# VectorE instead of GpSimd makes the low parts of the converted float64 weights

## The chip, the cores and the metric

One core of one Trainium2 chip runs the kernel. The metric is the device time of one execution in microseconds (us); a profiled execution has a span (first to last instruction of the program) and its own device time, which is a little longer.

## What is computed

A linear attention over 8 batches and 8 heads, followed by an MLP-mixer block:

```python
def phi(x):                       # x: q or k, (8, 8, 576, 64); w_phi: (64, 128)
    proj = einsum('bhsd,df->bhsf', x, w_phi)
    proj = proj - max(abs(proj), axis=-1)
    return concatenate([exp(proj), exp(-proj)], axis=-1)
kv  = einsum('bhsf,bhsd->bhfd', phi(k), v);  z = phi(k).sum(axis=2)
x   = einsum('bhsf,bhfd->bhsd', phi(q), kv) / (phi(q)·z + 1e-6)   # -> (8, 576, 512)
h   = relu(x^T @ w_tok1) @ w_tok2                    # 576 -> 256 -> 576
u   = x + h^T
out = u + relu(u @ w_ch1) @ w_ch2                    # 512 -> 1536 -> 512
```

The four MLP weights arrive as float64. Everything else is float32.

## The kernel before

**Split numbers.** Most products are made of float32r parts: a number is cast to float32r (the high part `hi`, on ScalarE or another engine), and the low part is `lo = raw - hi`. `mm3` (L70) then makes three matmuls, high by high, high by low, low by high. `split` (L62) is the helper that makes both parts: line L65 is the cast on ScalarE, L68 the subtraction, on the engine that the caller names.

**Weights.** `load_weights` (L137) calls `convert` once for each block of a weight: 7 blocks for `w1` and `w2` (tiles `bits`, `w_h`, `w_l`), 12 blocks of 128x512 for `wc1` (tiles `bitsc`, `wc_h`, `wc_l`) and 12 of 128x512 for `wc2` (tiles `bitsc`, `wc`: both parts lie in one tile). `convert` (L107) loads the 64-bit words with a DMA on SyncE's queue (L118) into one of four staging buffers, and turns them into float32 with integer operations: the absolute value of the upper word on ScalarE (L124), then on VectorE a clamp (L125), a shift and mask (L126), the sign and exponent (L127) and the three bits out of the lower word (L128). L125 and L126 read one tensor, `m`, the `bits` tile of the pool; L127 and L128 read two, the loaded words and `m`. `split` follows. The `bits` tile has three buffers, and one is free again when its low part has been subtracted.

**Streams.** Five generators are woven by `weave` (L547) into one program: `keys` and `queries` (the attention, one pair of heads at a time), `token_stream` (the token mix of a batch, when its attention is done), `load_weights` and `channel_stream` (18 blocks of 256 tokens). The first four pairs of heads (`i < PLAIN`) go through plain float32 matmuls, and VectorE takes their maxima (L219) and differences (`pmk`, `pmq`, L221) straight out of PSUM. From the fifth pair on the difference is GpSimd's (L221, `eng = nc.gpsimd`), and so are the low parts of keys and queries (L180), half of the low parts of the query features (L357), the division of the numerators (L402) and the low parts of the mixer's input (L470). The denominators of the first eight pairs make a round trip through DRAM (L394 to L399) with a reciprocal on VectorE between (L396).

**Order.** The kernel is built with the tile framework and `schedule_with_timeline_sim=True`: the framework plans the order of each engine's instructions by its own timeline before the launch, from the order of the woven program and the dependences; semaphores are added to that order. On the chip each engine works its list in order. In the trace the operations of up to three `convert` calls alternate on VectorE with those of the attention.

Of the kernel before, what the change touches and what calls it, by code (L numbers as in the profile page):

```python
# [8 lines left out]
F32 = mybir.dt.float32  # L9
# [33 lines left out]
def mixer_kernel(ctx, tc, qk, vm, vt, w_phi, w1, w2, wc1, wc2d, out):  # L43
    nc = tc.nc
# [17 lines left out]
    def split(hi, lo, raw, eng_hi, eng_lo):  # L62

        if eng_hi is nc.scalar:
            nc.scalar.copy(hi, raw)  # L65
        else:
            eng_hi.tensor_copy(hi, raw)
        eng_lo.tensor_tensor(lo, raw, hi.bitcast(F32), op=ALU.subtract)  # L68
# [38 lines left out]
    def convert(hi, lo, srcs, name, tag=None):  # L107

        w, n = hi.shape
        if tag is None:  # L110
            tag = f"late{nstage[0] % STAGES}"
            nstage[0] += 1
        raw = wk.tile([P, 4, 256], U32, tag=tag, name=f"raw{name}", bufs=3 if tag == "xt1" else 1)
        raw = raw.rearrange("p a b -> p (a b)")[:w, :2 * n]
        at = 0
        for src in srcs:
            m = src.shape[1]
            nc.sync.dma_start(raw[:, 2 * at:2 * (at + m)].bitcast(I64), src)  # L118
            at += m
        raw = raw.rearrange("p (n two) -> p n two", two=2)  # L120
        top, low = raw[:, :, 1], raw[:, :, 0]
        m = wk.tile([P, 512], U32, tag="bits", name=f"bits{name}", bufs=3)[:w, :n]

        nc.scalar.activation(m.bitcast(F32), top.bitcast(F32), AF.Abs)  # L124
        nc.vector.tensor_scalar(m.bitcast(F32), m.bitcast(F32), LEAST, MOST, op0=ALU.max, op1=ALU.min)  # L125
        nc.vector.tensor_scalar(m, m, 3, 0x3FFFFFF8, op0=ALU.logical_shift_left, op1=ALU.bitwise_and)  # L126
        nc.vector.scalar_tensor_tensor(m, top, 0xC0000000, m, op0=ALU.bitwise_and, op1=ALU.bitwise_or)  # L127
        nc.vector.scalar_tensor_tensor(m, low, 29, m, op0=ALU.logical_shift_right, op1=ALU.bitwise_or)  # L128
        split(hi, lo, m.bitcast(F32), nc.scalar, nc.gpsimd)

    def flat(t):
        return t.rearrange("p a b -> p (a b)")
# [4 lines left out]
    def load_weights():  # L137
        for u in (0, 3):
            s = UNITS[u][2]
            convert(flat(w1_h[:, u:u + 2]), flat(w1_l[:, u:u + 2]),  # L140
                    [w1[s + o:s + o + P] for o in (0, P)], f"1_{u}")
            yield 1.0
        convert(w1_h[:D, 2], w1_l[:D, 2], [w1[512:]], "1_2")
        for w in (w1_h, w1_l):
            nc.scalar.copy(w[D:, 2], w[:D, 2].bitcast(F32))
        yield 0.4
        for u in range(NT):
            rows = w2[u * P:(u + 1) * P]
            convert(w2_h[:, u, :256], w2_l[:, u, :256], [rows[:, :256]], f"2_{u}")
            yield 0.5  # L150
            convert(w2_h[:, u, 256:], w2_l[:, u, 256:], [rows[:, 512:], rows[:, 256:512]], f"3_{u}")
            yield 0.7
# [457 lines left out]
```

## Time and profile before

| | |
|---|---|
| device time, three runs | 1168.47, 1168.24, 1161.84 us (median 1168.24) |
| profiled execution: device time / span | 1164.33 / 1162.2 us |
| PE busy (matmul) | 1121.3 us, 96% of the span, 9032 matmuls |
| DVE / ACT / POOL busy | 685.7 / 659.4 / 570.1 us (59 / 57 / 49%) |
| chain that ended last, by engine | PE 85%, ACT 5%, DVE 4%, DMA 3%, issue 1%, POOL 1% |
| granted TensorE clock, mean | 0.992 |

PE is TensorE, PEld its weight load, DVE VectorE, ACT ScalarE, POOL GpSimd, SP SyncE. L12 is line 12 of the kernel. Times within the span count from its start. A name before the arrow is the tile that is written, names behind it are the tiles that are read.

### The profile page before, as it was taken

The page shows a single profiled execution, that of the slowest core. Times are in us where ns is not written, and L with a number is a line of the kernel's source. Part 1 is how long each engine was busy: PE and PEld are TensorE (multiplying, and loading weights), DVE is VectorE, ACT ScalarE, POOL GpSimd, SP SyncE. Part 2 cuts the span into 40 slices and gives each one's busy share as a digit, 9 for nine tenths or more (in the row PEclk, how much of TensorE's full clock was granted, in tenths as well). Part 3 has the DMA queues.
Part 4 walks back from the last instruction along what each step waited for, and adds up shares of the span by engine and source line. Part 5 has one row for each costly group of instructions (what it writes and reads, how often), then busy time and mean ns, then how long its engine had stood idle before and what let it go on. Part 6 is the DMA issues. An engine that isn't in the chain of part 4 may idle for free.

```text
span 1162.2 us, 24135 instructions
## 1 busy us (share of the span) xinstructions
PE 1121.3 (96%) x9032; PEld 1090.5 (94%) x9032; DVE 685.7 (59%) x1446; ACT 659.4 (57%) x1845; POOL 570.1 (49%) x734
## 2 busy tenths in 40 slices
PE   8987799999999999999999999999999999999998
PEld 7766699998999899999999999999999989999998
DVE  7989763536656665667566465573666666553111
ACT  5678785666656665666657465563655666441110
POOL 3347773555545564566646354563554655430000
PEclk9988999999999999999999999999999999999999
DMA  8564130111111011111111011110111110000000
GB/s 224 162 187 135 42 88 24 47 43 54 32 28 52 21 41 41 32 49 32 32 49 33 19 32 50 32 50 13 38 48 33 50 31 11 20 1 19 19 19 19
DMA packets 72531, 56.77 MB, mean 49 GB/s; under 512 B 49920, under 2 KB 63648, under 8 KB 72416
## 3 DMA queue, kind: packets, MB, share of 16 engines
q1 hardware_dynamic: 71056, 54.89, 16.7%
q8 instruction: 71, 1.16, 0.4%
q10 hardware_dynamic: 1360, 0.36, 0.2%
q14 instruction: 44, 0.36, 0.1%
HBM read 45.72 MB, written 9.51 MB: 48 GB/s over the span
## 4 chain that ended last, share of the span: by engine, by line
PE 85%; ACT 5%; DVE 4%; DMA 3%; issue 1%; POOL 1%; SPq 0%; POOLq 0%; DVEq 0%; ACTq 0%
PE acc L74 25%; PE h L74 25%; PE pkv L287 9%; PE pn L74 7%; PE ph L74 4%; PE pa L74 3%; PE pt L343 3%; PE ppk L205 2%; PE ppq L205 2%; DMA inv<-few 1%; PE px L423 1%; PE pn L377 1%; PE ppk L209 1%; ACT qh L356 1%; ACT qf L350 1%
## 5 line engine op out<-in xcount | busy, mean ns | idle before, releaser
L74 PE MATMUL acc<-gh,wc 128*128 128x256 f32 x1728 | 336.5, 282 | 0.2 <-ACT gh L489 0.2
L74 PEld LDWEIGHTS acc<-gh,wc 128*128 128x128 f32 x1728 | 274.0, 189 | 0.5 <-ACT gh L489 0.4
L74 PE MATMUL h<-ul,wc_h 128*128 128x256 f32 x864 | 243.4, 282 | 1.9 <-POOL ul L470 1.8
L74 PE MATMUL h<-uh,wc_h 128*128 128x256 f32 x864 | 244.8, 284 | 0.5 <-DVE gl L490 0.5
L74 PE MATMUL h<-uh,wc_l 128*128 128x256 f32 x864 | 243.7, 282 | 0.0
L74 PE MATMUL acc<-gl,wc 128*128 128x256 f32 x864 | 242.3, 282 | 0.0
L287 PE MATMUL pkv<-v,kp 128*128 128x65 f32 (+1 forms) x1152 | 165.7, 280 | 0.4 <-ACT kp L265 0.3
L74 PEld LDWEIGHTS h<-ul,wc_h 128*128 128x128 f32 x864 | 163.1, 189 | 2.7 <-POOL ul L470 2.7
L74 PEld LDWEIGHTS h<-uh,wc_h 128*128 128x128 f32 x864 | 162.6, 188 | 1.2 <-DVE gl L490 1.1
L74 PEld LDWEIGHTS h<-uh,wc_l 128*128 128x128 f32 x864 | 163.4, 189 | 0.0
L74 PEld LDWEIGHTS acc<-gl,wc 128*128 128x128 f32 x864 | 162.8, 188 | 0.0
L287 PEld LDWEIGHTS pkv<-v,kp 128*128 128x128 f32 x1152 | 156.9, 203 | 4.0 <-issue 1.8
L265 ACT ACTIVATE kp<-pmk 128x256 f32<-128x256 f32 (+1 forms) x320 | 109.3, 392 | 89.0 <-POOL pmk L221 83.7
L357 POOL TENSOR_TENSOR ql<-qf,qh 128x320 fp32r<-128x320 f32 (+1 forms) x112 | 92.8, 828 | 135.9 <-ACT qh L356 133.2
L490 DVE SCALAR_TENSOR_TENSOR gl<-h,gh 128x512 fp32r<-128x512 f32 x108 | 74.0, 686 | 140.3 <-ACT gh L489 139.6
L350 ACT ACTIVATE qf<-pt 128x320 f32<-128x320 f32 (+1 forms) x256 | 105.2, 414 | 84.6 <-PE pt L343 83.9
L489 ACT ACTIVATE gh<-h 128x512 fp32r<-128x512 f32 x108 | 64.6, 598 | 102.5 <-PE h L74 101.8
L74 PE MATMUL pn<-qh,kv 128*128 128x320 f32 (+1 forms) x448 | 114.9, 297 | 1.7 <-DVE pq L214 0.8
L402 POOL TENSOR_TENSOR xt<-xt,den 128x320 f32<-128x320 f32 x64 | 53.8, 840 | 116.7 <-DVE den L401 36.6
L357 DVE TENSOR_TENSOR ql<-qf,qh 128x320 fp32r<-128x320 f32 (+1 forms) x112 | 71.1, 635 | 65.0 <-ACT qh L356 64.6
L221 POOL TENSOR_TENSOR pmk<-pk,mxk 128x256 f32<-128x256 f32 (+1 forms) x140 | 86.8, 620 | 30.0 <-DVE mxk L219 23.2
L180 POOL TENSOR_TENSOR stq<-raw,stq 64x512 fp32r<-64x512 f32 (+1 forms) x56 | 79.8, 1424 | 40.5 <-ACT stq L179 36.4
(109 smaller groups left out, 2420.8 us busy)
## 6 DMA issues: line engine op xcount, KB each, us to landing
raw<-in_qk SPq DMA_DIRECT2D x27, 576.0 KB, 4.0
rawc<-in_wc SPq DMA_DIRECT2D x24, 512.0 KB, 4.8
v<-in_vm SPq DMA_DIRECT2D x31, 256.0 KB, 3.9
out_x<-xt SPq DMA_DIRECT2D x12, 256.0 KB, 2.2
out_x<-xt SPq DMA_DIRECT2D x16, 192.0 KB, 2.0
raw<-in_w SPq DMA_DIRECT2D x8, 256.0 KB, 3.5
out_x<-xt SPq DMA_DIRECT2D x16, 128.0 KB, 3.0
pair<-in_qk SPq DMA_DIRECT2D x8, 160.0 KB, 3.8
```

What stands on the lines that cost most here:

```text
L74: nc.tensor.matmul(o, a, m, start=first and i == 0, stop=last and i == 2, skip_group_check=group_ok)
L180: nc.gpsimd.tensor_tensor(t[lo:lo + D], src, t[base:base + D].bitcast(F32), op=ALU.subtract)
L205: nc.tensor.matmul(ps[:, i].rearrange("p two f -> p (two f)"), t[:, c:c + P], wp2.rearrange("p two f -> p (two f)"), start=True, stop=True)
L221: eng.tensor_tensor(pm[:, :n], pr, mx[:, :n].unsqueeze(2).to_broadcast([P, n, F]), op=ALU.subtract)
L265: nc.scalar.activation(kp[:, :len(us), sg], pm[:, :len(us)], AF.Exp, scale=1.0 - 2.0 * sg)
L287: nc.tensor.matmul(o, kp[:, n, sg], v, start=g == 0 and n == 0 and sg == 0, stop=u is None, skip_group_check=True)
L343: nc.tensor.transpose(ptr[:, n], r, ident)
L350: nc.scalar.activation(full, src, AF.Exp, scale=1.0 - 2.0 * sg)
L357: (nc.gpsimd if sg else nc.vector).tensor_tensor(lo, full, hi.bitcast(F32), op=ALU.subtract)
L402: nc.gpsimd.tensor_tensor(x, x, den, op=ALU.mult)
L489: nc.scalar.activation(gh, ph, AF.Relu)
L490: nc.vector.scalar_tensor_tensor(gl, ph, 0.0, gh.bitcast(F32), op0=ALU.max, op1=ALU.subtract)
```

## The change

In `convert`, the engine that `split` is given for the low part is VectorE instead of GpSimd. All 31 subtractions of L68 for weights move; their operands and results, and every other operation, stay as they were. The program is planned anew by the framework, since one of its instructions has another engine.

```diff
         nc.vector.scalar_tensor_tensor(m, low, 29, m, op0=ALU.logical_shift_right, op1=ALU.bitwise_or)
-        split(hi, lo, m.bitcast(F32), nc.scalar, nc.gpsimd)
+        split(hi, lo, m.bitcast(F32), nc.scalar, nc.vector)
```

## Rows read from the trace of the kernel before

**Rows 1.** Windows: stretch, length, busy us of PE, PEld, DVE, ACT, POOL, clock, DMA.

```profile
9.00:66.00 57.00, 56.70 (x234) 46.36 (x234) 52.07 (x118) 38.72 (x96) 21.52 (x16) 1.00 0.71 197
66.00:125.00 59.00, 45.85 (x250) 37.52 (x251) 55.62 (x102) 45.77 (x112) 36.84 (x30) 0.87 0.51 142
125.00:165.00 40.00, 35.84 (x275) 33.54 (x274) 25.86 (x64) 32.02 (x90) 30.42 (x38) 0.98 0.19 52
165.00:1162.00 997.00, 977.91 (x8258) 968.67 (x8257) 548.53 (x1153) 540.15 (x1545) 479.85 (x637) 1.00 0.12 33
```

**Rows 2.** The chain that ended last, 66 to 125 us: start, us, what.

```profile
75.36 3.92 DMA inv<-few
...
90.99 1.68 POOL wc L68
...
102.35 1.63 DVE bitsc L126
...
109.37 1.42 DVE bitsc L128
```

**Rows 3.** Groups by shape on DVE, 66 to 125 us: busy us, mean ns, idle before.

```profile
L128 DVE SCALAR_TENSOR_TENSOR bitsc<-rawc,bitsc 128x512 uint32<-128x512 uint32 x14 | 13.4, 959 | 0.0
L126 DVE TENSOR_SCALAR bitsc<-bitsc 128x512 uint32<-128x512 uint32 x13 | 11.4, 877 | 0.0
L127 DVE SCALAR_TENSOR_TENSOR bitsc<-rawc,bitsc 128x512 uint32<-128x512 uint32 x13 | 10.8, 831 | 0.0
L125 DVE TENSOR_SCALAR bitsc<-bitsc 128x512 f32<-128x512 f32 x13 | 8.7, 679 | 2.3 <-ACT bitsc L124 2.3
```

**Rows 4.** Tile bitsc, whole span: duration ns min/median/max, first and last start.

```profile
L126 DVE TENSOR_SCALAR bitsc<-bitsc x24: 408/424/1751, 28.9 to 156.3; 128x512 uint32<-128x512 uint32 x24
...
L128 DVE SCALAR_TENSOR_TENSOR bitsc<-rawc,bitsc x24: 645/680/1751, 31.7 to 158.2; 128x512 uint32<-128x512 uint32 x24
```

**Rows 5.** Timeline of DVE, then of POOL: start, us, engine, line.

```profile
84.80 0.69 DVE L128 SCALAR_TENSOR_TENSOR bitsc<-rawc,bitsc 128x512 uint32<-128x512 uint32 x1
85.40 0.42 DVE L126 TENSOR_SCALAR bitsc<-bitsc 128x512 uint32<-128x512 uint32 x1
...
102.27 1.71 DVE L126 TENSOR_SCALAR bitsc<-bitsc 128x512 uint32<-128x512 uint32 x1
...
102.16 1.54 POOL L180 TENSOR_TENSOR stq<-raw,stq 64x640 fp32r<-64x640 f32 x1 [1.36 <-ACT stq L179]
```

**Rows 6.** Groups by shape on POOL, 66 to 125 us.

```profile
L68 POOL TENSOR_TENSOR wc_l<-bitsc,wc_h 128x512 fp32r<-128x512 f32 x8 | 11.6, 1452 | 9.5 <-ACT wc_h L65 9.4
L68 POOL TENSOR_TENSOR wc<-bitsc,wc 128x512 fp32r<-128x512 f32 x5 | 6.9, 1379 | 1.7 <-ACT wc L65 1.6
```

**Rows 7.** Waits of DVE and POOL, 66 to 125 us: total us, times, longest.

```profile
DVE bitsc L125 <- ACT bitsc L124: 2.3, 3, 1.2
...
POOL wc_l L68 <- ACT wc_h L65: 9.4, 4, 2.9
...
POOL wc L68 <- ACT wc L65: 1.6, 2, 1.3
```

**Rows 8.** Windows of L68 alone: DVE busy, POOL busy, clock, DMA.

```profile
9.00:66.00 57.00, 0.00 (x0) 20.66 (x15) 1.00 0.71 197
...
125.00:165.00 40.00, 1.68 (x4) 3.86 (x3) 0.98 0.19 52
```

**Rows 9.** Waits of POOL, 9 to 66 us.

```profile
POOL wc L68 <- ACT wc L65: 9.2, 4, 4.2
POOL wc_l L68 <- ACT wc_h L65: 8.1, 3, 3.6
```

**Rows 10.** Timeline of PE: the two longest gaps between 66 and 125 us.

```profile
74.76 0.48 PE L209 MATMUL ppt<-wp,pair 64*128 64x128 f32 x2 [3.42 <-DVE pmq L221]
...
91.92 0.74 PE L209 MATMUL ppq<-wp,pair 64*128 64x128 f32 x4 [3.69 <-DVE pmq L221]
```

## The prediction

> **What bounds the kernel now.** I read the busy shares first, then the busy time by stretch, because a share over the whole span says nothing about the one stage that the change touches. The subtractions that move all start within the first 162 us. The windows [rows 1] show four stages. From 9 to 66 us PE is busy 56.70 of 57.00 us, and DVE 52.07. From 66 to 125 us PE falls to 45.85 of 59.00 us while DVE is busy 55.62, and TensorE's granted clock is 0.87 instead of 1.00: this is VectorE's stage. From 125 to 165 us no engine is full (PE 35.84, POOL 30.42, DVE 25.86 of 40.00). From 165 us to the end PE is busy 977.91 of 997.00 us, and since its work there stays the same, the end of the kernel is set by how much of PE's work the first 165 us could not place. So the change can act only through PE's idle time before 165 us: 59.00 − 45.85 = 13.2 us in VectorE's stage, 4.2 us behind it, next to nothing in the first stage. The chain of waits [rows 2] agrees: in 66 to 125 us it goes over denominators' round trips through DRAM, bit operations on DVE, and once over a moved operation, 1.68 us of POOL.
>
> The next view is the groups by shape in VectorE's stage against the quickest operations of the same shape. The 53 bit operations there took 13.4 + 11.4 + 10.8 + 8.7 = 44.3 us [rows 3]. Undisturbed ones take about 0.42 us (L125 and L126) and 0.68 us (L127 and L128), the medians [rows 4]; 26 x 0.42 + 27 x 0.68 = 29.3 us. So 15.0 us of VectorE's 55.62 is stretch. The timeline shows its source: a POOL subtraction started at 102.16 and took 1.54 us, and DVE's L126, started 0.11 us later, took 1.71 instead of 0.42, ending 0.28 us behind POOL [rows 5]. GpSimd's work on SBUF holds these DVE operations up.
>
> **The change part by part.**
>
> *Added to DVE.* No low part of a weight is on DVE in the trace. The nearest rows are L127 and L128, also two tensors in SBUF, 128x512: 0.68 us busy, and start to start 0.60 us where the next operation is ready (84.80 to 85.40 [rows 5]). I take 0.60 for each; at 0.68 the sum below grows by 1.0. Thirteen lie in VectorE's stage [rows 6]: +7.8 us there.
>
> *Removed stretch.* POOL is busy 36.84 us in this stage, of which the thirteen L68 are 11.6 + 6.9 = 18.5 us, one half [rows 1, 6]. I give them half of the stretch: −7.5 us. The bounds: nothing, if the remaining POOL work (which now starts earlier) meets DVE as often, and −15.0, if all of it was theirs.
>
> *New stretch.* The moved operations read two tensors in SBUF, as L127 and L128 do, so the rest of POOL's work can hold them up as well. That rest makes the other 7.5 us of stretch on 53 operations, 0.14 us each; 13 x 0.14 = +1.8 us (from 0 to 13 x 0.28 = 3.7, if stretch per operation stayed at today's 15.0 / 53).
>
> The Trainium skill, page "SBUF — State Buffer", section "SBUF: two separate sides", says that VectorE and GpSimd share one port pair as an exclusive lock, that a DVE operation with two SBUF inputs or in a two-port mode contends for it, and that whoever starts first holds it for the whole instruction. The rows at 102.16 and 102.27 agree [rows 5]. It speaks against counting the removed stretch as clear gain, since the subtraction stays a contender on its new engine; a result that the rule would allow is the second rival.
>
> *A new wait on DVE.* The subtraction needs ScalarE's cast (L65), which needs L128: a trip from DVE to ACT and back. DVE works in order, so behind a waiting L68 are queued the next bit operations and the maxima and differences (L219, L221) for which PE waits. The nearest DVE row is L125, which waits for ACT's L124: 2.3 us for thirteen [rows 7], so I take +2.3 us. It is so little because DVE has a backlog and the planner puts other work between. The other end is what POOL waits for the same cast today, 9.4 + 1.6 = 11.0 us for thirteen [rows 7]; POOL is less loaded and arrives earlier, hence DVE's row, but the end stays in the range. The lower end is 0.
>
> *Taken from POOL.* 18.5 us of work in this stage. Behind it in POOL's list stand the low parts of keys and queries (L180), L402 and L221. POOL idles 22 of 59 us, so most of this was not in the way; the one L68 in the chain is 1.68 us [rows 2]: −1.7 us (0 to −1.7). No DMA is issued by POOL here and the moved operation issues none; SyncE's load of the next block waits for L127 and L128, not for the subtraction. The `bits` buffer, freed by the subtraction, now comes free in DVE's order; ScalarE's L124 is what would wait.
>
> *Sum in VectorE's stage:* 7.8 − 7.5 + 1.8 + 2.3 − 1.7 = +2.7 us.
>
> *First stage, 9 to 66 us.* Fifteen move, among them seven smaller ones; at 0.60 at most +9.0 us, against the stretch that leaves with 20.66 us of POOL's 21.52 [rows 1, 8]. By VectorE's stage's ratio (15.0 us of stretch for 36.84 of POOL, 0.41) that is −8.4. Net +0.6, covered by PE's full stage and DVE's 4.9 us of idle time: 0. Were no stretch to leave, 9.0 − 4.9 = 4.1 us would show, the upper end; the lower end is −1, for PE has hardly a gap to give back.
>
> *Third stage.* Three move, +1.8 us on a DVE that is idle 14 of 40 us, −3.86 us on POOL, which is busy three quarters [rows 1, 8]. I take 0, between −3.9 and +1.8.
>
> *Behind 165 us* nothing moves, but the framework plans the whole program anew. PE's idle time there is 19.1 us; a third of it either way, ±6 us, is my bound for another order.
>
> The sum is +2.7 us on the profiled execution, 1164.33 to 1167.0. That execution lies 3.9 us under the median of the three runs, 1168.24; on the median the sum is 1170.9. I take the middle base, 1166.3, for everything: **1169 us**. Its own range, 1160 to 1177, has the re-planning and the bounds of the smaller terms.
>
> **Rivals.**
>
> *DVE is held at its head by ScalarE (slower).* If DVE comes to each L68 about as early as POOL does now, it inherits the 11.0 us instead of 2.3 in VectorE's stage: 1166.3 + 2.7 + 8.7 = 1177.7. In the first stage it would inherit 9.2 + 8.1 = 17.3 us [rows 9], of which 4.9 fit in its idle time: up to +12.4 more, 1190. The middle is 1184. It decides from about 0.5 us of wait for each operation on. For it: the trip to ACT is real, ACT is busy 45.77 of 59 us there and works in order. Against it: the small wait of L125 [rows 7].
>
> *POOL leaves more than its half (faster).* The removed operations hold DVE for their whole length, 18.5 us, not 7.5: −11.0 more, 1166.3 + 2.7 − 11.0 = 1158.0. (The lock that the Trainium skill's page "SBUF — State Buffer" states, section "SBUF: two separate sides", would allow this.) DVE's maxima would then come sooner, and PE's two long gaps, 3.42 and 3.69 us, both ended by `pmq` on DVE [rows 10], may close: down to 1150.9. I name 1155. Against it: the stretch that is there in all is 15.0 us, and the moved work takes 7.8 itself.
>
> *The new plan decides, the stage comes out even.* Moved work and stretch cancel, DVE's wait is nothing, and only the order behind 165 us differs: 1166.3 ± 6, 1160 to 1172. This is also the case where the change shows nothing.
>
> **How the numbers follow.** Forecast 0.48; DVE held by ScalarE 0.24; more from POOL's leaving 0.16; new plan alone 0.12. A measurement of this kernel can tell 1% from no change, 11.7 us: below 1156.6 is faster, above 1179.9 slower. Of the second rival two thirds lie below, 0.11, with 0.02 from the others: faster 0.13. Of the first rival three quarters lie above, 0.18, with 0.03 from the forecast's tail (both ends of the unknown waits together): slower 0.21. The rest, 0.66, is the same. The range leaves out a tenth on each side: the lower half of the second rival and the upper part of the first, 1154 to 1186.
>
> **What would show it.** In the changed profile, L125 to L128 in VectorE's stage should be at a mean near 0.55 to 0.75 us instead of 0.68 to 0.96; a DVE group of 24 L68 with mean 0.68 to 0.85 us; its idle time before, ended by ACT's L65, under 5 us in all (over 15 is the first rival); DVE still above 90% busy from 66 to 125 us; POOL's other subtractions unchanged in length; PE full from about 167 us on. The prediction is wrong if DVE idles in front of L68, if the stretch of the bit operations stays or disappears whole, or if PE's idle time behind 165 us differs by more than 6 us.

## The result and the profile after

The changed kernel took 1175.22 us (median of 20 runs, 1164.64 to 1180.82), the kernel before 1168.36 (20 runs). The ratio is 1.0071, 95% interval 1.0047 to 1.0095: slower by 0.7%, some 7 to 8 us. In a second comparison (`changed_again` below) the ratio was 1.0115 (1.0074 to 1.0155).

The profiled execution of the changed kernel took 1164.77 us with a span of 1163.0 us, at the quick end of its runs. So its rows show what moved, but not the loss. On its page PE has 1112.6 us (96%), DVE 693.9, ACT 657.6, POOL 528.6.

Windows of the changed kernel, the same stretches and columns as [rows 1]:

```profile
9.00:66.00 57.00, 54.65 (x289) 43.90 (x290) 49.99 (x130) 42.97 (x111) 5.27 (x5) 0.97 0.67 175
66.00:125.00 59.00, 42.74 (x253) 35.49 (x253) 53.13 (x112) 42.56 (x109) 20.72 (x23) 0.93 0.50 150
125.00:165.00 40.00, 33.29 (x208) 30.71 (x207) 37.67 (x70) 26.61 (x70) 21.12 (x23) 0.80 0.22 67
165.00:1162.00 997.00, 976.75 (x8266) 967.33 (x8265) 549.51 (x1157) 542.70 (x1552) 480.09 (x639) 1.00 0.12 33
```

Against [rows 1], TensorE does 289 matmuls instead of 234 in the first stage, about as many in the second, and 208 instead of 275 in the third. (A second execution of the same program did 261, 214 and 173, so single counts are rough.) VectorE is busier in the third stage (37.67 us instead of 25.86) and less busy in the first two (103.1 instead of 107.7). The change left no conversion work out; it is done later.

DVE groups by shape, 66 to 125 us, which answer to [rows 3], and the moved subtraction with its counts, durations (min/median/max ns) and the waits ahead of it:

```profile
L127 DVE SCALAR_TENSOR_TENSOR bitsc<-rawc,bitsc 128x512 uint32<-128x512 uint32 x12 | 9.4, 787 | 0.0
L128 DVE SCALAR_TENSOR_TENSOR bitsc<-rawc,bitsc 128x512 uint32<-128x512 uint32 x12 | 8.8, 732 | 0.0
L125 DVE TENSOR_SCALAR bitsc<-bitsc 128x512 f32<-128x512 f32 x11 | 7.2, 657 | 0.4 <-ACT bitsc L124 0.4
L126 DVE TENSOR_SCALAR bitsc<-bitsc 128x512 uint32<-128x512 uint32 x12 | 6.8, 570 | 0.0
```

```profile
L68 DVE TENSOR_TENSOR wc_l<-bitsc,wc_h x12: 644/682/1509, 38.0 to 138.9; 128x512 fp32r<-128x512 f32 x12
L68 DVE TENSOR_TENSOR wc<-bitsc,wc x12: 672/684/1609, 60.0 to 159.2; 128x512 fp32r<-128x512 f32 x12
...
  ACT xh L65: 34.8, 33
  ACT wc L65: 0.8, 2
```

The bit operations are shorter than in [rows 3], by 22 (L125) to 307 ns (L126). The subtraction takes 0.68 us on VectorE where GpSimd took 1.38 to 1.45 [rows 6], and the cast keeps VectorE waiting for 0.8 us in all (the 34.8 us above it belong to another use of the helper, `xh`). By these rows alone the change looks like a small gain. The experiments had to find where the loss comes from.

### The profile page after: what moved, and what is told of

It reads as the page before. It is cut to its first block, busy times and chain, and to the rows that moved or that the text cites. A ratio compares the mean times of both kernels' runs of the same rounds, so it can differ in the third digit from the quotient of the medians.

```text
span 1163.0 us, 24116 instructions
## 1 busy us (share of the span) xinstructions
PE 1112.6 (96%) x9032; PEld 1081.7 (93%) x9032; DVE 693.9 (60%) x1477; ACT 657.6 (57%) x1845; POOL 528.6 (45%) x703
## 4 chain that ended last, share of the span: by engine, by line
PE 82%; DVE 5%; ACT 5%; DMA 4%; issue 1%; POOL 1%; SPq 1%; DVEq 0%; POOLq 0%; ACTq 0%
PE acc L74 25%; PE h L74 24%; PE pkv L287 9%; PE pn L74 7%; PE ph L74 4%; PE pt L343 3%; PE pa L74 2%; PE ppk L205 2%; PE ppq L205 2%; DMA few<-row 2%; DMA inv<-few 1%; PE px L423 1%; PE ppk L209 1%; DMA den<-inv 1%; PE pn L377 1%
## 5 line engine op out<-in xcount | busy, mean ns | idle before, releaser
L287 PE MATMUL pkv<-v,kp 128*128 128x65 f32 (+1 forms) x1152 | 161.1, 275 | 3.2 <-ACT kp L265 2.3
L287 PEld LDWEIGHTS pkv<-v,kp 128*128 128x128 f32 x1152 | 152.0, 198 | 6.7 <-ACT kp L265 2.9
L350 ACT ACTIVATE qf<-pt 128x320 f32<-128x320 f32 (+1 forms) x256 | 105.2, 415 | 80.0 <-PE pt L343 78.6
L221 POOL TENSOR_TENSOR pmk<-pk,mxk 128x256 f32<-128x256 f32 (+1 forms) x140 | 86.6, 619 | 34.0 <-DVE mxk L219 27.9
```

The costliest lines, as they stand in the source:

```text
L221: eng.tensor_tensor(pm[:, :n], pr, mx[:, :n].unsqueeze(2).to_broadcast([P, n, F]), op=ALU.subtract)
L287: nc.tensor.matmul(o, kp[:, n, sg], v, start=g == 0 and n == 0 and sg == 0, stop=u is None, skip_group_check=True)
L350: nc.scalar.activation(full, src, AF.Exp, scale=1.0 - 2.0 * sg)
```

## Experiments

Two things change together: the engine of 31 subtractions, and the order that the framework plans for every engine. Read by line and tile from the two traces, TensorE's list of matmuls differs from the old one at some 820 of its 9032 places, nearly all between the 73rd and the 1129th; the other engines' lists differ as well. To separate the two, a kernel builds the program twice: the first build gives each engine's order, and the second is bound to it, all but the 31 subtractions, by ordering edges that need no semaphore. This code, and the edits below, are shortened:

```python
order = program(on_gpsimd, lay)[1]        # whose plan is kept
nc = program(on_vector, lay, order)[0]    # who makes the low parts
...
for names in order.values():              # or one engine's list, or a part of it
    for first, then in zip(names, names[1:]):
        tc.add_manual_dep(made[then], first, NoSync)
```

In these kernels the subtraction on VectorE has line L611 and the cast of the weights L129; the other lines keep their numbers. The table holds all runs, and the change itself as `after`. Each was timed beside the kernel before; as the four timings of that kernel differ, runs are compared by their ratios. The last two columns are added up from the windows of each profiled execution: matmuls from 9 to 165 us, and VectorE's busy time from 9 to 125 us.

| run | low part | lists kept | median us | ratio (95%) | span | PE 9–165 | DVE 9–125 |
|---|---|---|---|---|---|---|---|
| before | GpSimd | own plan | 1162.73 to 1168.97 | 1 | 1162.2 | 759 | 107.7 |
| after | VectorE | own plan | 1175.22 | 1.0071 (1.0047–1.0095) | 1163.0 | 750 | 103.1 |
| changed_again | VectorE | own plan | 1178.44 | 1.0115 (1.0074–1.0155) | 1182.0 | 648 | 91.6 |
| vector_old_order | VectorE | all old | 1159.62 | 0.9958 (0.9925–0.9991) | 1157.8 | 768 | 109.6 |
| zero_low_old_order | none | all old | 1162.32 | 0.9970 (0.9947–0.9993) | 1157.3 | 789 | 102.4 |
| gpsimd_new_order | GpSimd | all new | 1177.34 | 1.0108 (1.0069–1.0147) | 1172.4 | 683 | 91.1 |
| vector_old_dve_list | VectorE | DVE old | 1178.07 | 1.0085 (1.0053–1.0117) | 1181.0 | 637 | 94.8 |
| vector_old_pe_list | VectorE | PE old | 1163.45 | 0.9958 (0.9932–0.9985) | 1164.6 | 761 | 105.2 |
| gpsimd_new_dve_list | GpSimd | DVE new | 1177.84 | 1.0075 (1.0047–1.0104) | 1177.4 | 657 | 89.6 |
| change_five_bits | VectorE | own plan | 1173.54 | 1.0052 (1.0023–1.0080) | 1174.9 | 673 | 101.1 |
| vector_old_pe_first200 | VectorE | PE old to 200 | 1164.55 | 1.0004 (0.9977–1.0031) | 1164.9 | 773 | 108.1 |
| vector_old_pe_from200 | VectorE | PE old from 200 | 1174.12 | 1.0080 (1.0053–1.0108) | 1170.0 | 670 | 97.2 |
| gpsimd_new_pe_list | GpSimd | PE new | 1179.50 | 1.0142 (1.0099–1.0185) | 1186.1 | 582 | 89.0 |
| replanned_before | GpSimd | own plan | 1173.23 | 1.0074 (1.0043–1.0104) | 1165.9 | 753 | 108.7 |

**Work or order.** The changed kernel once more, the work without the new order, the new order without the work, and the old order with no subtraction at all (that kernel leaves the low parts out: GpSimd writes zeros in their place).

changed_again:

> The change once more, to have it on one chip beside the next three. Both theories expect what was measured, +0.5 to +1.0% against the kernel before (+6 to +11 us), and TensorE's mean granted clock lower than in the kernel before by about 0.01.

vector_old_order, `order = program(on_gpsimd)`, `nc = program(on_vector, order)`:

> The 31 subtractions on VectorE, but every other instruction of every engine in the planned order of the kernel before; only the subtractions are placed anew. Theory A (the work: 0.6 us for each on VectorE outweighs the stretch that leaves) expects +6 to +11 us against before, as for the change. Theory B (the order: the new plan loses the time, the work is even) expects within 3 us of before. My forecast of the sum, work alone, was +2.7 us.

gpsimd_new_order, against vector_old_order:

```diff
-    order = program(on_gpsimd, lay)[1]
-    nc = program(on_vector, lay, order)[0]
+    order = program(on_vector, lay)[1]
+    nc = program(on_gpsimd, lay, order)[0]
```

> The subtractions on GpSimd as before, every other instruction in the planned order of the changed kernel. Theory A expects before's time within 3 us; theory B expects +6 to +11 us. If both parts matter, this and the run with the old order add up to the change.

zero_low_old_order, against vector_old_order:

```diff
-    return [nc.vector.tensor_tensor(lo, raw, hi, op=ALU.subtract).ins.name]
+    return [nc.gpsimd.memset(lo.bitcast(F32), 0.0).ins.name]
```

> Leaves the subtraction out: the low parts of the weights are filled with zeros by GpSimd, which reads nothing in SBUF for that; the order of everything else is that of the kernel before. It prices the stretch alone. By my split (half of 15.0 us in VectorE's stage, about 8 us in the first stage) the bit operations L125 to L128 should lose some 15 us in all, and the kernel 5 to 10 us. If the stretch is taken over by the rest of GpSimd's work, within 3 us of before.

The work alone is no loss: 0.9958. The order alone, with the subtraction still on GpSimd, costs 1.0108. Multiplied, they give 1.0065; the change measured 1.0071, and 1.0115 (1.0074 to 1.0155) in the comparison that these runs belong to. Leaving the subtraction out saves no more (0.9970, or 3.5 us, less than the 5 to 10 that my split of the stretch gave) than moving it. Between 66 and 125 us its 57 bit operations take 39.4 us where 31.5 would be undisturbed: 7.9 us of stretch, about as much as with the move (below).

Windows of the work in the old order:

```profile
9.00:66.00 57.00, 52.48 (x257) 42.64 (x258) 54.40 (x141) 42.05 (x104) 2.13 (x2) 0.88 0.75 208
66.00:125.00 59.00, 45.99 (x242) 38.39 (x242) 55.23 (x116) 45.76 (x112) 23.52 (x21) 0.83 0.47 134
125.00:165.00 40.00, 36.31 (x269) 33.91 (x268) 25.47 (x61) 30.18 (x84) 25.84 (x33) 0.95 0.18 48
```

DVE groups of the same kernel, 66 to 125 us, and its waits for the cast between 9 and 165 us (us, times, longest):

```profile
L127 DVE SCALAR_TENSOR_TENSOR bitsc<-rawc,bitsc 128x512 uint32<-128x512 uint32 x13 | 11.2, 864 | 0.0
L128 DVE SCALAR_TENSOR_TENSOR bitsc<-rawc,bitsc 128x512 uint32<-128x512 uint32 x13 | 10.3, 789 | 0.0
L126 DVE TENSOR_SCALAR bitsc<-bitsc 128x512 uint32<-128x512 uint32 x13 | 7.6, 586 | 0.0
L125 DVE TENSOR_SCALAR bitsc<-bitsc 128x512 f32<-128x512 f32 x12 | 6.7, 562 | 0.2
L611 DVE TENSOR_TENSOR wc_l<-bitsc,wc_h 128x512 fp32r<-128x512 f32 x7 | 4.8, 681 | 0.0
L611 DVE TENSOR_TENSOR wc<-bitsc,wc 128x512 fp32r<-128x512 f32 x7 | 4.8, 680 | 1.8 <-ACT wc L129 1.8
```

```profile
DVE wc L611 <- ACT wc L129: 1.8, 1, 1.8
```

Here the forecast's terms can be read one by one (below).

**Which list.** I first suspected VectorE's list, because the new plan puts the conversions later: of the L128 operations it has 17 ahead of the last of the 40 maxima that read PSUM directly (L219), the old plan 25 by its trace. The rival was TensorE's list. Each was kept by itself while the rest was planned around it. A fourth kernel let the conversions run further ahead, with five `bits` buffers instead of three in the changed kernel.

vector_old_dve_list and vector_old_pe_list:

```diff
-        for names in order.values():
+        for names in [order["DVE"]]:      # or [order["PE"]]
```

> The subtractions on VectorE; of the old order only VectorE's own list is kept, the four other engines are planned anew. In VectorE's old list 26 of the 31 conversions are done (L128) ahead of the 40th maximum (L219), in the changed kernel's list 17. Theory C (the new plan loses by putting the conversions later on VectorE) expects what the whole old order gave, within 3 us of 1160 us (-5 to -8 us against before). Theory D (the order of the other engines, PE's above all) expects the changed kernel's +6 to +11 us.

> The subtractions on VectorE; of the old order only PE's list is kept. In VectorE's list, planned anew under that, 22 conversions stand ahead of the 40th maximum. Theory C expects a time between, about before's (-3 to +4 us). Theory D, if PE's list is the cause, expects the whole gain of the old order, -5 to -8 us.

gpsimd_new_dve_list, the new list of VectorE with the subtraction on GpSimd:

> The subtractions on GpSimd as before; only VectorE's list is that of the changed kernel (17 conversions ahead of the 40th maximum), the other engines are planned anew. Theory C expects the loss of the whole new order, +8 to +13 us. Theory D expects within 3 us of before.

change_five_bits:

```diff
-        m = wk.tile([P, 512], U32, tag="bits", name=f"bits{name}", bufs=3)[:w, :n]
+        m = wk.tile([P, 512], U32, tag="bits", name=f"bits{name}", bufs=5)[:w, :n]
```

> The change with five instead of three buffers for the tile bits, planned freely. With the subtraction on VectorE a buffer is held for longer in the plan, and the next conversion can begin only when one is free; with five the plan puts 19 conversions ahead of the 40th maximum instead of 17. Theory C expects a little of the loss back: +3 to +8 us against before. If the buffers are the whole cause of the late conversions, before's time or better.

With VectorE's old list, conversions early again, the kernel stayed slow (1.0085): my first suspicion falls. With TensorE's old list alone it was as quick as with all lists old (0.9958). The slow gpsimd_new_dve_list (1.0075) tells little, because TensorE's list was planned anew there as well. Five buffers gave 1.0052, an interval that overlaps the change's.

**Which part of TensorE's list, and whether any new order costs.** The 200th matmul starts at 57 us in the kernel before; what it and those ahead of it do is attention alone.

vector_old_pe_first200 and vector_old_pe_from200:

```diff
-        for names in order.values():
+        for names in [order["PE"][:200]]:     # or [order["PE"][200:]]
```

> The subtraction on VectorE as in the change; only the first 200 matmuls of TensorE keep the old order (up to about where token mixing begins), everything else is planned anew. Theory D1 (the early part of TensorE's list costs the time): 1160 to 1166 us, as with the whole old list of TensorE. Theory D2 (the part behind it costs it): 1172 to 1180 us, as with the change.

> The subtraction on VectorE; TensorE keeps the old order from its 200th matmul on, the first 200 and all other engines are planned anew. D1: 1172 to 1180 us. D2: 1160 to 1166 us.

gpsimd_new_pe_list:

> The subtraction on GpSimd as in the kernel before; only TensorE's list is that of the change, the other engines are planned around it. Theory D (TensorE's order is the cause): the whole loss, 8 to 12 us over the kernel before. If TensorE's order costs only together with the other lists: within 3 us of the kernel before.

replanned_before, the kernel before with a nudge to the planner:

```diff
-            (load_weights(), 10.0, False), (channel_stream(), 19.5, False)])
+            (load_weights(), 10.1, False), (channel_stream(), 19.5, False)])
```

> The kernel before with one weight of the planner's weaving moved from 10.0 to 10.1, no instruction added or removed, so that only the order is another. If this program's time moves with any new order: 3 to 12 us away from the kernel before, to either side. If only the order that the change brought is a bad one by a mechanism of the change: within 3 us.

The first 200 places decide: old ones with everything else planned anew give 1.0004, new ones with the old list behind them 1.0080. TensorE's new list with the subtraction on GpSimd gives the whole loss, 1.0142. The nudge, which adds and removes nothing, gave 1.0074, as much as the change itself. So my narrower reading, that only the order that the change brought is a bad one, does not hold: another new order of the same program costs as much. But that order is new elsewhere: by the traces, TensorE's list is the old one for its first 912 places, up to 181 us, and the other engines' lists differ only behind 190 us.

Windows of vector_old_pe_first200, then of vector_old_pe_from200:

```profile
9.00:66.00 57.00, 52.00 (x261) 42.09 (x261) 51.83 (x137) 41.64 (x104) 3.21 (x3) 0.92 0.72 195
66.00:125.00 59.00, 46.60 (x251) 37.76 (x251) 56.30 (x117) 45.67 (x113) 23.97 (x22) 0.88 0.52 148
125.00:165.00 40.00, 36.71 (x261) 34.12 (x262) 27.16 (x62) 30.45 (x84) 25.72 (x31) 0.92 0.17 44
```

```profile
9.00:66.00 57.00, 53.79 (x281) 42.74 (x281) 49.66 (x130) 42.54 (x110) 5.70 (x5) 0.97 0.67 177
66.00:125.00 59.00, 48.80 (x224) 39.51 (x225) 47.52 (x99) 39.43 (x98) 19.06 (x18) 0.70 0.46 139
125.00:165.00 40.00, 31.07 (x165) 28.77 (x165) 35.56 (x69) 27.08 (x70) 20.69 (x24) 0.68 0.27 82
```

The reader should see three things in the second fence. The new order is ahead at 66 us, with 281 matmuls against 261. It then falls behind by 27 and 96. And in the stage that VectorE used to bound, VectorE is busy 47.52 us instead of 56.30 while the granted clock is 0.70 instead of 0.88: the bound has shifted towards TensorE. The waits of VectorE, 9 to 125 us, first of vector_old_pe_first200, then of gpsimd_new_pe_list, the slowest, show for whom it waits:

```profile
DVE few L396 <- DMA few<-row: 2.3, 2, 2.1
...
DVE mxt L219 <- PE ppt L209: 1.1, 1, 1.1
DVE mxk L219 <- PE ppq L209: 0.7, 1, 0.7
```

```profile
DVE mxq L219 <- PE ppq L209: 10.0, 8, 2.1
DVE mxk L219 <- PE ppk L209: 9.4, 6, 3.6
DVE mxt L219 <- PE ppt L209: 2.4, 2, 1.3
DVE pmq L221 <- PE pt L343: 2.1, 4, 1.0
```

VectorE waits about 2 us for TensorE in the first and 23.9 in the second (21.8 of it for projections). By the same sum it is 11.2 us in vector_old_pe_from200, 16.3 in changed_again, but 3.1 in the quick profiled execution of the change, and 4.6 in the kernel before. A maximum that waits at VectorE's head holds the bit operations queued behind it; what is not converted by 125 us is done in the third stage, where in the kernel before only one of the 24 L128 of `wc1` and `wc2` was left; in vector_old_pe_from200 there are eight.

## Why the prediction came out as it did

The time was 1175.22 against a forecast of 1169, slower as forecast, inside its range and within 1%. But the +2.7 us that were to make it slower did not; two errors of opposite sign met, and that the number came so close is luck. None of the prediction's signs of being wrong appeared in the profile of the change: the one for another order looked behind 165 us, and the loss lies ahead of it.

- *Added work, removed and new stretch, the wait.* In vector_old_order the stage from 66 to 125 us has 14 subtractions of 0.68 us, 9.5 us; the forecast had 7.8 + 1.8 = 9.6 for thirteen. The 51 bit operations take 35.8 us; undisturbed, 25 x 0.42 + 26 x 0.68 = 28.2 by the medians [rows 4], so 7.6 us of stretch is left of 15.0 and −7.4 went, against −7.5. The wait for the cast is 1.8 us against 2.3. These terms held, though single profiles with a few operations at each edge do not carry tenths. The share of the removed stretch was a plain half, a guess, and half it was. The −1.7 us taken from GpSimd no run prices by itself.
- *The first rival*, VectorE held at its head by ScalarE, falls: 0.8 us in the changed kernel, 1.8 in the old order, against the 11.0 that it needed in this stage alone [rows 7].
- *The second rival*, all 18.5 us of GpSimd's work leaving VectorE, falls too: 7.6 us of stretch stayed. The lock that the Trainium skill states (page "SBUF — State Buffer", section "SBUF: two separate sides") shows in [rows 5], but GpSimd's busy time is not VectorE's loss one for one: 18.5 us of subtractions left GpSimd, its busy time in the stage fell by 13.3 us (36.84 to 23.52, other work moved in), and 7.4 us of stretch went.
- *The first stage, put at 0*, rested on "PE's full stage", a reading of [rows 1] that does not carry over: busy 56.70 of 57 us, but with 234 matmuls, and up to 58 us each at the longer of its two durations (last section). In the old order with the work moved TensorE does 257 in the same stretch, and L125 and L126 there fell from 576 and 769 ns to 423 and 422. A share of busy time did not show that TensorE could do more. How much of this the missing stretch gives is not shown: with the same order and no subtraction at all TensorE did 220 (first line), and a second execution of the changed kernel 261 (second line) instead of 289.

```profile
9.00:66.00 57.00, 48.78 (x220) 39.80 (x220) 48.99 (x120) 36.14 (x91) 6.18 (x12) 0.88 0.66 186
9.00:66.00 57.00, 52.45 (x261) 42.60 (x261) 45.22 (x122) 38.16 (x99) 2.71 (x3) 0.98 0.63 164
```

- *The sum, +2.7 us.* The work in the old order came to −0.42% (−0.75 to −0.09), and to the same with only TensorE's list kept; with the lists planned anew behind the first 200 matmuls it came to +0.04% (−0.23 to +0.31). That is nothing to a small gain, where the sum had a loss of 0.23%. Which of its terms is off by these few us stays open.
- *The new plan, put at ±6 us behind 165 us*, is the step that failed. The new order alone costs 0.0108 x 1167.3 = 12.6 us (8.1 to 17.2), and nearly all of it early: in all 14 profiles the time from the 1000th matmul to the end is 968 to 975 us, while that matmul starts at 188.5 to 193.2 us in the profiles with a span under 1167 us and at 201.3 to 216.2 us in the others. The third rival ("the new plan decides") had the right cause, with the place and half the size wrong. For replanned_before, whose lists differ only behind 181 us, place and size were closer: at 165 us it is only 6 matmuls behind the kernel before (753 against 759), and loses more between 165 and 282 us, as the windows of before and then of replanned_before show:

```profile
165.00:282.00 117.00, 112.90 (x939) 110.76 (x939) 54.44 (x130) 73.75 (x211) 63.43 (x85) 1.00 0.16 43
282.00:1150.00 868.00, 856.77 (x7253) 849.88 (x7252) 492.02 (x1020) 465.80 (x1334) 416.42 (x553) 1.00 0.11 32
```

```profile
165.00:282.00 117.00, 112.79 (x908) 109.61 (x907) 50.28 (x124) 71.01 (x204) 58.70 (x80) 0.97 0.16 42
282.00:1150.00 868.00, 856.04 (x7263) 849.10 (x7263) 496.64 (x1028) 468.70 (x1344) 421.15 (x559) 1.00 0.11 32
```

What is shown: TensorE's order in its first 200 matmuls, with the plans that follow from it, carries the loss of the change. What stays open: why that order is the worse one, and why the nudge's order, new only behind 181 us, is.

In the 14 profiles the loss goes with TensorE's clock. Ahead of 190 us TensorE has 56 to 75 us at its lower level (1.2 of 2.4 GHz, the start without a clock record counted in) where the 1000th matmul starts by 193.2 us, and 85 to 121 us where it starts later. It does so within one program too, whose order is the same in every execution. The profiled execution of the changed kernel (clock 0.93 and 0.80 in the second and third stage, span 1163.0) and changed_again (0.73 and 0.82 there, span 1182.0) are one program. Of the 79 executions of the kernel before that were timed beside the experiments, 45 have a mean granted clock of 0.981 or more (where I part them) and a median of 1162.6 us, 34 a lower clock and 1171.3 us. With TensorE's first 200 places old and the work moved or left out, 45 of 48 executions are on the higher side; in the runs with those places new 3 of 59 are, in the changed kernel 4 of 20, in replanned_before 5 of 12. So much of what the ratios show is how often an execution has the lower clock. Whether the clock is the cause there, or follows from waits that differ between executions, is not told apart.

The version to keep is the change without its new plan: 1159.62 us with all lists old, quicker than the kernel before by 0.42% (0.09 to 0.75) and than the change by more than 1%.

## What to carry to other kernels

Where a framework plans the order from the program, a change of one engine is two changes; bind the old order and time the work by itself before you judge it, and nudge the planner once to learn what another order can be worth (here 0.7%, more than the work). A stage in which an engine is busy all the time is full only if its operations have their shortest durations there: compare counts and mean durations before you call a term covered. A gain of this size is kept by keeping the order, not by the edit alone.

## What the runs showed of the hardware

Matmuls of one shape have two durations. In the profile of the kernel before they ran at the longer one up to 58 us, although the clock printed there is 1.00 [rows 1]. Groups of TensorE by shape: first of before, 30 to 57 us (printed clock 1.00); then of vector_old_pe_from200, 30 to 57 us (1.00); then of the same, 66 to 100 us (0.56):

```profile
L209 PE MATMUL ppk<-wp,pair 64*128 64x128 f32 x18 | 5.3, 454 | 0.0
L209 PE MATMUL ppq<-wp,pair 64*128 64x128 f32 x16 | 4.5, 448 | 0.0
```

```profile
L209 PE MATMUL ppk<-wp,pair 64*128 64x128 f32 x34 | 5.9, 296 | 0.0
L209 PE MATMUL ppq<-wp,pair 64*128 64x128 f32 x28 | 4.7, 294 | 0.0
```

```profile
L209 PE MATMUL ppq<-wp,pair 64*128 64x128 f32 x16 | 4.9, 458 | 0.1
```

The durations of the first fence are those of the third, where the clock is near its lower level (1.2 of 2.4 GHz), not of the second. The 1.00 of the first is no measurement: the clock records of that trace begin at 58.3 us, with the upper level, and a stretch without a record is printed as 1.00. In the other 13 profiles they begin at 27.9 to 39.6 us, and in all 14 the `ppq` matmuls of this shape last 452 to 461 ns between 9 and 30 us. So the 1.00 that the prediction set against 0.87 in VectorE's stage was for the most part no reading, and at the start of a kernel the duration of a known shape tells the speed of TensorE, not the printed clock. Executions of one program on one chip were also up to 15 us apart (1163.57 to 1178.55 for replanned_before), twice what the change is worth, which is why single profiles here locate a loss but do not size it.
